# Key weights in blocks of 128 rows, first sums on two engines, and a new order for a transformer layer on one core

## The chip, the cores and the metric

The kernel runs on one core of a Trainium2 chip. The metric is the device time of one execution in microseconds (us); lower is better. The engines are TensorE (PE in the profile), VectorE (DVE), ScalarE (ACT), GpSimd (POOL) and SyncE (SP). SP, and here at the start ACT too, issue the DMAs that move data between the chip's main memory and the on-chip buffers; a name with q behind it, such as SPq, is the queue of that engine.

## The reference

A layer normalisation, an attention whose features are softmaxes, an output projection with a residual, and a gated feed-forward with a second residual, on x of 2048 rows and 448 columns in bf16:

```python
# A: x is layer-normalised first; 16 heads of 28
q, k, v = heads(x @ wqkv)
pq, pk = q @ w_phi, k @ w_phi                    # per head
phi_q = concat(softmax(pq), softmax(-pq))        # 28 + 28 features
phi_k = concat(softmax(pk), softmax(-pk))
kv, z = sum_s phi_k v, sum_s phi_k
o = (phi_q kv) / (phi_q z + 1e-6)
h = x + o @ wo
# B: h is layer-normalised first
h2 = h + (sigmoid(hn @ w_gate) * (hn @ w_up)) @ w_down     # 1792 inner columns
```

## The kernel before

The 2048 rows are 16 tiles of 128 rows (t = 0 to 15), or eight pairs of tiles (pr). All work is cut into named tasks. Each task has an engine, or a short list of engines that may run it, a function that issues its instructions, and the names of the tasks that it needs. A planner would order them by cost, but here the order is written out: `ORDER` is a table of some 900 numbers. The number divided by 32 is the place of a task among all tasks as they are declared; the last two bits choose among the task's engines, and three bits in between choose PSUM banks. `stored` decodes the table, and `emit` gives each engine its tasks in that order, with a semaphore wait wherever a task needs a result of another engine. So each engine, and each DMA queue, works strictly in its own order, and a task that waits holds all that stands behind it on its engine.

The stages, with the task names used below:

- Loads. `x,t` loads tiles of x (two or four at a time), `wk` the key weights, `wph` the feature weights, `wv` the value weights, `wq` the query weights (four pieces), `wom` the output weights (eight pieces). `wg`, `wu`, `wd` are the feed-forward weights and come later, each waiting for the one two places earlier.
- Weights. `kT` transposes the key weights on PE (four tasks of four transposes, line 537), `WkT` copies each result out of PSUM, `wM,1` multiplies it with the feature weights `Wp` (line 553), and `W2,1` casts the folded key weights back. The query weights go the same way, but their transpose is a DMA (`wqT`, line 499), followed by `wM,0` and `W2,0`.
- Normalisation of x. `bst` (line 581) and `agg` are the statistics, `ve` and `rstd` the inverse deviation (the power runs on POOL), `mm` and `nm` a helper for ACT, `xn` (lines 600 and 601) writes the normalised tile. Tiles 0 to 3 are transposed on PE (`xP`, line 611) and copied (`xT`); the others, in pairs, by DMA (`xT`, line 619, on SP).
- Keys and values. `pa` and `pb` are the two parts of a tile's key and value products (line 635; for tiles 0 and 1 the value products are `va`, `vb`). `ekp` and `ekm` are exponentials on ACT (lines 655, 657), `v1` copies the values. `sa` (line 665) adds the two halves of the exponentials' features in each group, from 896 to 448 elements in f32; `ss` sums further, `rs` inverts, `phi` (line 681) scales. `kv` adds the tile's part to a PSUM bank that `kv0` starts.
- Queries: `qa`, `q` (line 733) and the exponentials `eqp`, `eqm` (line 743), for 512 rows at a time.
- After `kvz`, which masks the finished sums: `num` (line 769), its copy `ocp`, then `rSm`, `rr`, `b`, `c`, `rd`, `o` on DVE for a pair, the transposes `oT` (by DMA on SP, line 818, behind `od`, or for pair 0 on PE as `oP`), the projection `woa`, `wo_` (line 830), the residual (`h`, or `hc` for pair 0, whose residual is added in PSUM by `wr`), the second statistics, `hn`, and its transposes `hT`.
- Feed-forward in five chunks of 2, 4, 4, 4 and 2 tiles: `ga`, `gu` (line 931), `sig` on ACT, `hh` on DVE, `dn` (line 965), `fin` and the store `st`.

At the start PE has nothing to do while data comes. It then runs `fill` tasks, matmuls of zeros (line 985). There are 17, and `ORDER` places them: 13 ahead of the first transposes and four between the later ones. The key weights arrive as one load of four blocks of 112 rows:

```python
load("wk", wk_raw[:], A_wqkv[:, D:2 * D].rearrange("(a p) n -> p a n", p=GP), bias=BIG, size=392.0,
     engs=("act", "sp"))
```

Of the kernel before, what the change touches and what calls it, by code (L numbers as in the profile page):

```python
# [5 lines left out]
dt = mybir.dt  # L6
# [4 lines left out]
P = 128  # L11
D = 448
H = 16
DH = 28
G = 4
HL = 4
GP = 112
KT = 4
# [13 lines left out]
NWARM = 1  # L32
NFILL = 17
# [62 lines left out]
class _Graph:  # L96
# [29 lines left out]
    def opt(self, name):  # L126
        return name if name in self.tasks else None
# [194 lines left out]
def build(nc, A_x, A_wqkv, A_w_phi, A_wo, B_w_gate, B_w_up, B_w_down, out):  # L322
# [16 lines left out]
    NXP, NEK, NPHI, NV, NOP, NO, NHP, NSG, NSA = 8, 4, 3, 4, 3, 2, 2, 4, 2  # L339
    SPLIT = range(NT)  # L340

    with ExitStack() as es:
# [8 lines left out]
        WkT = sb("WkT", [P, KT, D])  # L351
# [10 lines left out]
        ident = sb("ident", [P, P])  # L362
# [5 lines left out]
        warm = sb("warm", [P, P])  # L368
# [29 lines left out]
        o_pad = sb("o_pad", [P, NO, 2, 512])  # L398
        oT = sb("oT", [P, NO, 2, G, P])
        wk_raw = nc.alloc_sbuf_tensor_at("wk_raw", [GP, G, D], dt.bfloat16, offset=nc.lookup_mloc(o_pad).addr)  # L400
# [7 lines left out]
        bank16 = {b: a.bitcast(dt.bfloat16) for b, a in bank.items()}  # L408
# [3 lines left out]
        task, opt = K.task, K.opt  # L412
# [47 lines left out]
        def load(name, dst, src, eng="sp", deps=(), bias=0.0, size=0.0, behind=(), engs=None):  # L460
            task(name, eng, 0.55 if eng == "sp" else 0.6, lambda e: e.dma_start(dst, src), deps, lat=0.9, kind="in",
                 bias=bias, size=size, behind=behind, engs=engs)
# [7 lines left out]
        BIG = 2000.0  # L470
# [7 lines left out]
        def rows_of(w, c0, n, half_):  # L478
# [4 lines left out]
        load("wk", wk_raw[:], A_wqkv[:, D:2 * D].rearrange("(a p) n -> p a n", p=GP), bias=BIG, size=392.0,  # L483
             engs=("act", "sp"))
        load("wph", wphd[:], A_w_phi.rearrange("h i j -> (h i) j").rearrange("(a p) j -> p a j", p=GP), bias=BIG - 1,
             size=30.0)
        for h_ in range(2):
            load(("wv", h_), Wv[:, 2 * h_:2 * h_ + 2, :], rows_of(A_wqkv, 2 * D, D, h_), bias=BIG - 4 - h_, size=224.0,
                 engs=("act", "sp"))
# [43 lines left out]
        for b in range(G):  # L533
            def f(e, b=b):
                bk = got(("kT", b))[0]
                for k in range(G):
                    r = e.transpose(bank16[bk][0:GP, k * GP:(k + 1) * GP], wk_raw[:, k, b * GP:(b + 1) * GP],
                                    ident[0:GP, 0:GP])
                return r
            task(("kT", b), "pe", 0.3, f, ["wk", "ident", ("warm", NWARM - 1)], banks=ANY, until=[("WkT", b)], bias=950.0)  # L540
            task(("WkT", b), None, dve(D), lambda e, b=b: copy(
                e, WkT[0:GP, b, :], bank16[got(("kT", b))[0]][0:GP, 0:D]), [("kT", b)], bias=940.0,
                engs=("act", "dve") if b % 2 == 0 else ("dve", "act"))
# [109 lines left out]
        for t in range(NT):  # L653
# [10 lines left out]
            if t in SPLIT:  # L664
                task(("sa", t), "pool", 0.88, lambda e, t=t, s=s: e.tensor_tensor(  # L665
# [3 lines left out]
                    [("ekp", t), ("ekm", t), opt(("ss", t - NSA))])  # L669
# [356 lines left out]
```

## Time and profile before

| what | value |
|---|---|
| median of 3 runs | 208.35 us (208.34 to 208.68) |
| the profiled execution | 208.78 us, of which the span of the profile is 207.0 us |
| PE busy | 198.2 us, 96% of the span |
| DVE busy | 138.5 us, 67% |
| ACT busy | 94.9 us, 46% |
| POOL busy | 34.2 us, 16% |
| first key product (line 635) | starts at 12.35 us |
| mask of the finished sums, `kvz` | starts at 49.49 us |
| first feed-forward product (line 931) | starts at 67.77 us |
| last PE work ends | about 204.1 us |

The span is the stretch between the first and the last recorded event; the remaining 1.78 us of the profiled execution lie around it. A busy share is a mean over stages that differ: DVE, at 67%, is busy 4.9 of every 5 us between 5 and 40 us. PE counts the fillers as busy. In a timeline row the first number is the start, the second the duration of the row (of all its instructions, where an `x` and a count follow), and brackets give the idle time before it with what ended that.

### The profile page before, as it was taken

The page shows a single profiled execution, that of the slowest core. Times are in us where ns is not written, and L with a number is a line of the kernel's source. Part 1 is how long each engine was busy: PE and PEld are TensorE (multiplying, and loading weights), DVE is VectorE, ACT ScalarE, POOL GpSimd, SP SyncE. Part 2 cuts the span into 40 slices and gives each one's busy share as a digit, 9 for nine tenths or more (in the row PEclk, how much of TensorE's full clock was granted, in tenths as well). Part 3 has the DMA queues.
Part 4 walks back from the last instruction along what each step waited for, and adds up shares of the span by engine and source line. Part 5 has one row for each costly group of instructions (what it writes and reads, how often), then busy time and mean ns, then how long its engine had stood idle before and what let it go on. Part 6 is the DMA issues. An engine that isn't in the chain of part 4 may idle for free.

```text
span 207.0 us, 5437 instructions
## 1 busy us (share of the span) xinstructions
PE 198.2 (96%) x2281; PEld 106.6 (51%) x2281; DVE 138.5 (67%) x318; ACT 94.9 (46%) x166; POOL 34.2 (16%) x56
## 2 busy tenths in 40 slices
PE   7799988999898999999999999999999999999994
PEld 2444545555444887444444444544444455796553
DVE  2999999987999999379895655434744332462042
ACT  2399799889998944343411234003243320252000
POOL 5628763740001030002100101000100000000000
PEclk9999999999999999999999999999999999999999
DMA  6989896953027568600722000700050000000043
GB/s 189 288 155 150 176 222 165 232 182 92 3 51 54 73 134 155 118 0 19 130 52 54 0 3 8 144 1 3 2 139 3 0 2 3 0 3 0 3 142 124
DMA packets 35093, 16.94 MB, mean 82 GB/s; under 512 B 26812, under 2 KB 34044, under 8 KB 35068
## 3 DMA queue, kind: packets, MB, share of 16 engines
q1 hardware_dynamic: 34332, 15.96, 36.9%
q10 hardware_dynamic: 736, 0.63, 1.0%
q8 instruction: 18, 0.29, 0.6%
q14 instruction: 7, 0.06, 0.1%
HBM read 8.98 MB, written 1.84 MB: 52 GB/s over the span
## 4 chain that ended last, share of the span: by engine, by line
PE 72%; DVE 15%; DMA 6%; ACT 3%; issue 1%; POOL 1%; POOLq 0%; ACTq 0%
PE bank L931 38%; PE bank L965 18%; PE bank L635 6%; DMA oT<-o_pad 5%; PE bank L830 3%; PE bank L733 3%; DVE st L581 2%; PE bank L693 2%; DVE xn_pad L601 2%; DMA x_sb<-in_A_x_dram 2%; DVE phi L681 1%; DVE o_pad L797 1%; DVE b_sb L792 1%; DVE b_sb L789 1%; PE bank L769 1%
## 5 line engine op out<-in xcount | busy, mean ns | idle before, releaser
L931 PE MATMUL bank<-xnT,wg_sb 64*128 64x512 bf16 (+1 forms) x490 | 87.7, 333 | 0.0
L931 PE MATMUL bank<-xnT,wu_sb 64*128 64x512 bf16 (+1 forms) x490 | 87.7, 333 | 0.0
L940 ACT ACTIVATE sg_sb<-bank 128x512 f32<-128x512 f32 (+1 forms) x70 | 34.6, 511 | 82.7 <-PE bank L931 78.2
L948 DVE SCALAR_TENSOR_TENSOR hh<-sg_sb,bank 128x512 bf16<-128x512 f32 (+1 forms) x70 | 39.2, 575 | 34.7 <-ACT sg_sb L940 34.4
L931 PEld LDWEIGHTS bank<-xnT,wg_sb 64*128 64x128 bf16 x490 | 45.3, 94 | 20.1 <-issue 1.4
L931 PEld LDWEIGHTS bank<-xnT,wu_sb 64*128 64x128 bf16 x490 | 45.1, 94 | 16.8
L965 PE MATMUL bank<-wd_sb,hh 128*128 128x448 bf16 (+1 forms) x238 | 43.1, 342 | 0.0
L965 PEld LDWEIGHTS bank<-wd_sb,hh 128*128 128x128 bf16 x238 | 22.9, 98 | 20.1 <-issue 1.1
L972 DVE SCALAR_TENSOR_TENSOR x_sb<-bank,x_sb 128x448 bf16<-128x448 f32 (+1 forms) x17 | 9.8, 594 | 23.1 <-PE bank L965 23.1
L635 PE MATMUL bank<-Wk,xnT 64*128 64x448 bf16 x112 | 21.5, 350 | 0.1
L635 PE MATMUL bank<-Wv,xnT 64*128 64x448 bf16 x112 | 21.2, 350 | 0.0
L870 POOL TENSOR_TENSOR rs<-rs,neghalf 128x2 f32<-128x2 f32 x8 | 6.4, 805 | 87.4 <-DVE rs L868 87.2
L665 POOL TENSOR_TENSOR half_s<-ek 128x448 f32<-128x448 bf16 x16 | 16.7, 1056 | 13.8 <-ACT ek L657 6.0
L743 ACT ACTIVATE eq<-bank 128x1024 bf16<-128x1024 f32 x16 | 16.6, 1041 | 1.2 <-PE bank L733 0.9
L733 PE MATMUL bank<-xnT,Wq 64*128 64x512 bf16 x112 | 14.6, 377 | 0.8 <-DVE opm L425 0.5
L830 PE MATMUL bank<-wo_sb,oT 64*128 64x448 bf16 x112 | 13.3, 350 | 0.9 <-DMA oT<-o_pad 0.6
L425 ACT CAST opm<-bank 128x960 bf16<-128x960 f32 x14 | 13.1, 979 | 0.9 <-PE bank L769 0.8
L635 PEld LDWEIGHTS bank<-Wk,xnT 64*128 64x128 bf16 x112 | 9.4, 94 | 5.7 <-PE bank L635 0.5
L635 PEld LDWEIGHTS bank<-Wv,xnT 64*128 64x128 bf16 x112 | 9.4, 94 | 5.1 <-ACT ek L657 0.3
L581 DVE BATCH_NORM_STATS2 st<-x_sb 128x6 f32<-128x448 bf16 x16 | 9.3, 608 | 1.8 <-DMA x_sb<-in_A_x_dram 1.8
L681 DVE TENSOR_TENSOR phi<-ek,rsum 128x896 bf16<-128x896 bf16 x16 | 10.1, 653 | 0.1
L670 DVE TENSOR_REDUCE ssum<-half_s 128x32 f32<-128x448 f32 x16 | 9.7, 608 | 0.6 <-POOL half_s L665 0.5
(91 smaller groups left out, 177.6 us busy)
## 6 DMA issues: line engine op xcount, KB each, us to landing
wu_sb<-in_B_w_up_dram SPq DMA_DIRECT2D x4, 448.0 KB, 3.6
wg_sb<-in_B_w_gate_dram SPq DMA_DIRECT2D x4, 448.0 KB, 4.7
out_dram<-x_sb SPq DMA_DIRECT2D x15, 112.0 KB, 1.8
wd_sb<-in_B_w_down_dram SPq DMA_DIRECT2D x7, 224.0 KB, 3.6
x_sb<-in_A_x_dram SPq DMA_DIRECT2D x2, 448.0 KB, 5.6
x_sb<-in_A_x_dram SPq DMA_DIRECT2D x3, 224.0 KB, 4.2
wq_raw<-in_A_wqkv_dram SPq DMA_DIRECT2D x4, 128.0 KB, 5.1
Wv<-in_A_wqkv_dram SPq DMA_DIRECT2D x2, 224.0 KB, 5.2
```

The source lines that it names most:

```text
L425: return e.copy(dst, src) if hasattr(e, "activation") else e.tensor_copy(dst, src)
L581: task(("bst", t), "dve", dve(D), lambda e, t=t: e.bn_stats(st1[:, t % 4, :], X(t)), [x_ld[t], opt(("agg", t - 4))])
L635: r = e.matmul(bank[bk][:, 0:D], lhsT=half(xnT, hi)[:, t, k, :], rhs=half(w, hi)[:, k, :], start=(i == 0), stop=(i == 6), tile_position=(6 ...
L665: task(("sa", t), "pool", 0.88, lambda e, t=t, s=s: e.tensor_tensor(half_s[:, t % NSA].rearrange("p (a n) -> p a n", a=4 * G), ek[:, s].re ...
L681: task(("phi", t), None, 1.68, lambda e, t=t, s=s: e.tensor_tensor(phi[:, t % NPHI, :, :, 0:DH, :].rearrange("p a g d h -> p (a g) d h"), ...
L733: r = e.matmul(bank[bb[j]], lhsT=half(Wq2, hi)[:, k, 2 * g:2 * g + 2].rearrange("p c d h -> p (c d h)"), rhs=half(xnT, hi)[:, 4 * c:4 * c ...
L743: task((key, gp, c), "act", act_p(1024), lambda e, gp=gp, c=c, sg=sg, nm=nm: e.activation(eq[c][:, sg, 2 * gp:2 * gp + 2, :], wide[got(nm) ...
L830: r = e.matmul(bank[bb[j]][:, 0:D], lhsT=half(oT, hi)[:, pr % NO, j, k, :], rhs=half(wo_sb, hi)[:, k, :], start=(i == 0 and not res), stop ...
L931: r = e.matmul(bank[b][:, 0:N], lhsT=half(w, hi)[:, k, fs], rhs=half(hnT, hi)[:, t0:t0 + n, k, :], start=(i == 0), stop=(i == 6), tile_pos ...
L940: task(("sig", f_, c), "act", act_p(N), lambda e, j=j, N=N, nm=nm: e.activation(sg_sb[:, j % NSG, 0:N], bank[got(nm)[0]][:, 0:N], ACT.Tanh ...
L948: task(("hh", f_, c), "dve", dve(N), lambda e, j=j, N=N, nm=nm, f_=f_, c=c: e.scalar_tensor_tensor(hhT[c % 2][:, f_, 0:N], sg_sb[:, j % NS ...
L965: r = e.matmul(bank[b][:, c0:c1], lhsT=hhT[c % 2][:, f_, o:o + P], rhs=wd_sb[:, f_, c0:c1], start=(f_ == 0), stop=(f_ == FT - 1))
```

## The change

The key weights are loaded in blocks of 128 rows: three blocks in one load and the remaining 64 rows in a second. The tile `wk_raw` gets 128 partitions, and each `kT` transposes blocks of 128, 128, 128 and 64 rows instead of four of 112. `sa` may run on POOL or on DVE. `NFILL` falls from 17 to 14. `ORDER` is a new table, with new choices of engine.

```diff
-NFILL = 17
+NFILL = 14
...
-704 545 0 96 224 1120 320 736 352 576 28384 256 608 28416 480 384 28448 768 448 288 28480 800 128 160 28512
+544 576 0 480 1152 609 224 737 128 28416 160 640 96 28448 352 801 192 28480 768 256 448 28512 384 896 28544
...
-        wk_raw = nc.alloc_sbuf_tensor_at("wk_raw", [GP, G, D], dt.bfloat16, offset=nc.lookup_mloc(o_pad).addr)
+        wk_raw = nc.alloc_sbuf_tensor_at("wk_raw", [P, KT, D], dt.bfloat16, offset=nc.lookup_mloc(o_pad).addr)
...
-        load("wk", wk_raw[:], A_wqkv[:, D:2 * D].rearrange("(a p) n -> p a n", p=GP), bias=BIG, size=392.0,
-             engs=("act", "sp"))
+
+        load(("wk", 0), wk_raw[:, 0:3, :], A_wqkv[0:3 * P, D:2 * D].rearrange("(a p) n -> p a n", p=P), bias=BIG,
+             size=336.0, engs=("act", "sp"))
+        load(("wk", 1), wk_raw[0:64, 3, :], A_wqkv[3 * P:D, D:2 * D], bias=BIG, size=56.0, engs=("act", "sp"))
...
-                for k in range(G):
-                    r = e.transpose(bank16[bk][0:GP, k * GP:(k + 1) * GP], wk_raw[:, k, b * GP:(b + 1) * GP],
-                                    ident[0:GP, 0:GP])
+                for k in range(KT):
+                    m = min(P, D - k * P)
+                    r = e.transpose(bank16[bk][0:GP, k * P:k * P + m], wk_raw[0:m, k, b * GP:(b + 1) * GP], ident[0:m, 0:m])
...
-                task(("sa", t), "pool", 0.88, lambda e, t=t, s=s: e.tensor_tensor(
+                task(("sa", t), None, 0.88, lambda e, t=t, s=s: e.tensor_tensor(
...
-                    [("ekp", t), ("ekm", t), opt(("ss", t - NSA))])
+                    [("ekp", t), ("ekm", t), opt(("ss", t - NSA))],
+                    engs=("pool", "dve"))
```

What the new table does to the queues at the start, in the order of issue:

| queue | before | after |
|---|---|---|
| ACT, loads | `x,0`; `wk` | `wk,0`; `x,2`; `x,6` |
| SP, loads | `x,2`, `x,4`, `wph`, `x,6`, `x,8`, `wv,0`, `wq,2`, `wq,0`, `wom,3`, `wv,1`, `x,12` | `x,0`, `wk,1`, `wph`, `x,4`, `wq,0`, `wq,3`, `x,8`, `wq,2`, `wv,0`, `wv,1`, `wq,1`, `x,12` |
| SP, next | `xT,4`, `wq,3`, `wom,0`, `wq,1`, `xT,6`, `wqT,1`, `wqT,0`, `xT,8` | `wqT,1`, `wom,4`, `wqT,0`, `xT,4`, `xT,6`, `xT,8` |
| PE | 13 fillers, `xP,1`, `kT,0`, `kT,2`, `kT,1`, `xP,2`, `kT,3`, the four `wM,1` with one filler, `xP,0`, `xP,3`, three fillers, `pa,0` | 12 fillers, the four `kT`, `xP,1`, three `wM,1`, `xP,0`, `kv0`, the last `wM,1`, two fillers, `xP,2`, `xP,3`, `pa,0` |

Four of the 16 `sa` (tiles 6, 10, 12 and 15) are on DVE after the change. Other tasks change sides too: `W2,1,2`, `W2,0,1`, `W2,0,2`, `v1` of tiles 8, 9, 12 and 14, `xn` of tiles 6, 10 and 12 and the two `hT` copies of pair 0 go from DVE to ACT; `xT,1`, `v1` of tiles 0, 5 and 10 and `xn` of tiles 13 and 14 go from ACT to DVE. Lines behind the edits move by two or three: line 635 becomes 637, line 931 becomes 934.

More of the change, by code (lines that the diff above doesn't have):

```diff
@@ L535, in f @@
                 bk = got(("kT", b))[0]
-                for k in range(G):
-                    r = e.transpose(bank16[bk][0:GP, k * GP:(k + 1) * GP], wk_raw[:, k, b * GP:(b + 1) * GP],
-                                    ident[0:GP, 0:GP])
+                for k in range(KT):
+                    m = min(P, D - k * P)
+                    r = e.transpose(bank16[bk][0:GP, k * P:k * P + m], wk_raw[0:m, k, b * GP:(b + 1) * GP], ident[0:m, 0:m])
                 return r
-            task(("kT", b), "pe", 0.3, f, ["wk", "ident", ("warm", NWARM - 1)], banks=ANY, until=[("WkT", b)], bias=950.0)
+            task(("kT", b), "pe", 0.3, f, [("wk", 0), ("wk", 1), "ident", ("warm", NWARM - 1)], banks=ANY, until=[("WkT", b)], bias=950.0)
             task(("WkT", b), None, dve(D), lambda e, b=b: copy(
```

92 rows, old and new, of the table ORDER are left out of this document.

## The prediction

> **What bounds the kernel now.** I read the page first (engine shares by slice), then the timeline of each engine over the first 70 us, the waits of TensorE (PE), and the DMA issues with their landing times. 0.2% of the time, 0.42 us, is about what a measurement of this kernel can tell from no change.
>
> ```profile
> PE   7799988999898999999999999999999999999994
> DVE  2999999987999999379895655434744332462042
> ```
>
> These are slices of 5.2 us. From 68 us on PE is full (its 136 us of feed-forward work are the same instructions before and after). Earlier VectorE (DVE) is just as full, so time can only come from the first 68 us, and there from two engines at once. PE's timeline, start and duration in us:
>
> ```profile
> 1.44 5.71 PE L985 MATMUL bank<-warm 128*128 128x512 bf16 x13
> 7.90 0.40 PE L611 MATMUL bank<-ident,xn_pad 128*128 128x128 bf16 x4 [0.74 <-DVE xn_pad L601]
> 8.13 0.78 PE L537 MATMUL bank<-ident,wk_raw 112*112 112x112 bf16 x12
> 12.35 0.93 PE L635 MATMUL bank<-Wk,xnT 64*128 64x448 bf16 x8
> ```
>
> Fillers run to 7.15. PE then waits for the normalised tile 1, because its transpose stands ahead of the key weights' in the queue; the weights start at 8.13 and the first key product at 12.35. The weights themselves were issued at 1.29 and landed 5.4 later, at 6.69:
>
> ```profile
> wk_raw<-in_A_wqkv_dram ACTq DMA_DIRECT2D x1, 392.0 KB, 5.4
> ```
>
> From the waits of PE:
>
> ```profile
> PE bank L693 <- DVE phi L681: 1.0, 2, 0.6
> PE bank L553 <- DVE Wq L425: 0.5, 1, 0.5
> ```
>
> These are the stalls between 12.35 and the end of the key/value stage at 49.4: 0.40 at 21.92, 0.53 at 27.07, 0.60 at 31.65, together 1.53 us. Behind them stand delays of DVE:
>
> ```profile
> 19.07 2.32 POOL L665 TENSOR_TENSOR half_s<-ek 128x448 f32<-128x448 bf16 x2 [0.32 <-ACT ek L657]
> 19.50 1.06 DVE L601 TENSOR_SCALAR xn_pad<-x_sb,mv,rs 128x512 bf16<-128x512 bf16 x1
> 36.39 1.86 DVE L681 TENSOR_TENSOR phi<-ek,rsum 128x896 bf16<-128x896 bf16 x2
> ```
>
> A normalisation takes 0.40 alone and 1.06 here, while GpSimd (POOL) adds halves (`sa`). It recurs at 24.17 (+0.76), 29.17 (+0.64) and in the pair at 36.39 (1.86 against 1.10): 2.8 us of DVE in all. Last, the transposes of x by DMA on SP's queue:
>
> ```profile
> 12.95 1.33 SPq L619 DMA_TRANSPOSE xnT<-xn_pad  x1
> 18.68 2.86 SPq L499 DMA_TRANSPOSE WqT<-wq_raw  x2
> DMA to landing us min/median/max: 3.1/4.5/4.8
> ```
>
> The first one issued at 12.95 feeds the product of tile 4, which ran at 18.16 without a wait.
>
> **The change, part by part.**
>
> *Key weights and fillers.* `wk` becomes two loads. The built order puts the first (336 KB) at the head of ScalarE's (ACT) queue, but the second (56 KB) on SP's, behind `x,0`. On ACT's queue 630 KB before (`x,0`, `wk`) had landed at 6.69; now 344 KB at its head should land near 5.0. That alone buys nothing: `wk` was already in 0.46 before the old fillers ended. Twelve fillers instead of 13 stand ahead, at 0.43 each: PE is free at 6.7 instead of 7.15. What counts is that the four `kT` now stand ahead of `xP,1`: they start at 6.7, not 8.13 (1.4 earlier). The number of transposes and their columns are the same, up to 128 wide instead of 112, so their cost stays.
>
> *Up to the first key product.* ACT: four `WkT` copies (1.84) 7.0 to 8.9, four `W2` casts (0.48 each, one of them from DVE) to 10.8. DVE: `x,0` lands at 4.1 as the first load on SP did before, then 7 statistics at 0.54, 4 aggregations at 0.15, 4 normalisations at 0.37, one 0.17, and `xT,1` at 0.40 (now here, not on ACT): 6.4, plus 0.3 of waits for `x,2` and `x,6`, which now come behind `wk` (estimates 6.3 and 7.8 from the 630 KB at 6.69), so `xT,0` ends at 11.1. First product at 11.25 instead of 12.35: **-1.1**; bounds 10.9 (no wait for x) and 12.1 (`x,6` at 8.5 and no overlap).
>
> *Transposes on SP.* Both `wqT` (1.43 each to issue) now stand ahead of `xT,4`; `wqT,0` waits for `wq,1`, which lands near 12.1 (the first batch of some 3.0 MB was in by 12.2, when DMA fell idle; `wq,1` now stands ahead of its last 448 KB), so SP is free at about 13.4. That hides, because `xn,5`, which `xT,4` needs, comes later: DVE after 11.1 does a statistic, four aggregations, one 0.17, three statistics, one 0.16 and two normalisations, 3.6 in all: 14.7 against 12.95 before. Landing 4.7 later: 19.4. PE gets there at 18.2: 11.25 plus the products of tiles 0 to 3 (5.25), three query folds (0.8) and one `kv` (0.3), with 0.6 of waits for ACT's `ekm,3` and for `phi,0`. Old progress there: 18.16 plus the folds and the `kv`, 1.1, is 19.26; so the lead of 1.1 turns into 0.14 behind: **+1.2**; bounds 0.6 (landing after 4.1) and 2.2 (DVE held once more by POOL). Queued behind it on PE: `wM,0,3`, tiles 5 to 7. The later transposes gain: `xT,6` at 16.1 (17.32) and `xT,8` at 20.3 (21.64), since the `wqT` are out of their way.
>
> *First sums on either engine.* Four of 16 `sa` (tiles 6, 10, 12, 15) go to DVE: 448 elements there take 0.54 by the statistic's spacing (bounds 0.27, half of `phi`'s spacing for 896, and 0.62): +2.1 on DVE. Against that, over the key/value stage, DVE gives away `W2,1,2`, `W2,0,1`, `W2,0,2`, four `v1` (seven at 0.54), and a net handful of small ones, and takes `xT,1`, three `v1`: the sum is 41.5 us of DVE work before (16 each of statistics 0.54, aggregations 0.13, `ss` 0.53, `rs` 0.30 and `phi` 0.54, 10 normalisations at 0.36, 8 copies at 0.53, 1.0 of small ones) and 41.3 after. ACT gains 2.3 net; it had 3.7 idle between 15 and 50. POOL loses 4.2. With 12 `sa` left on POOL the 2.8 of delays would scale to 2.1.
>
> *Stalls.* With the weights folded earlier (`W2,0` on ACT) and `phi` no longer last, I take the three old stalls as gone: **-1.5**. The delays by POOL do not vanish, they fall elsewhere: **+0.5** on the path (0 to 1.5, what they cost before). [...]
>
> *Numerators to feed-forward.* On DVE `o,1` and `od,1` (0.75) move ahead of `oT`; the two `hT` copies (0.8) go to ACT. By the rows the feed-forward starts 18.4 after the mask `kvz`, 18.28 before: **+0.1** (0 to 0.6).
>
> *Feed-forward.* Same work; `oT,4` now has 4.5 us of PE work between its issue and its use (5.8 before), `oT,5` 4.5 (5.2), against landings of 3.1 to 4.8: **+0.15** (0 to 0.8). The tail keeps its order (two halves of tile 15): 0.
>
> Sum: -1.1 + 1.2 - 1.5 + 0.5 + 0.1 + 0.15 = **-0.65**. The profiled execution took 208.78 (span 207.0 and 1.78 around it), 0.43 above the median of 208.35. So a profiled run near 208.1 and a median of 207.7.
>
> **The rivals.**
>
> *DVE swallows it.* DVE carries 41.3 of work against 41.5 from the same start at 4.1; if the POOL delays stay at 2.8 and 0.6 of new waits come, `kvz` stays at 49.5 and the time at 208.35. For: DVE's slices are all 9s. Against: four fewer `sa` on POOL, and the waits of 0.29 and 0.54 late in the stage went with them. Chance 0.17.
>
> *The late transpose.* `xT,4` lands at 20.4 or later: `xn,5` meets the first `sa` on POOL (by my walk they start within 0.2 of each other), or the wire is still full, since `wq,1` and `wq,3` join the first batch. Then the wait is 2.2 or more and moves all products of tiles 4 to 7. With half of the old stalls left: -1.1 + 2.2 - 0.75 + 0.5 + 0.1 + 0.15 = +1.1, 209.4. It decides from a landing of about 20.0. Chance 0.22.
>
> *A slow TensorE.* The fillers start every 0.43, but four transposes take 0.40 at 7.90: PE was at half rate up to at least 6.6 and at full rate by 7.9. With fewer fillers the transposes and folds could run at half rate, +1.7 of PE work before and 1.3 in the first product: -0.65 + 1.3 = 209.0. The page's clock row (all 9s) does not show it. Chance 0.06. [...] Here 5.5 us of fillers had passed and the spacing was still 0.43.
>
> *Order in the feed-forward.* Two late `oT` cost over 1 us: 209.0. Chance 0.07.
>
> *All of the lead is kept.* `xT,4` early, no delay by POOL: -1.1 + 0.6 - 1.5 + 0.1 = -1.9, 206.45. Chance 0.10.
>
> **How the numbers follow.** The forecast has the remaining 0.38. Faster: 0.38 + 0.10 = 0.48; same 0.17; slower 0.22 + 0.06 + 0.07 = 0.35. Both signs hold much, so the forecast's own range is 207.1 to 207.9. The range of all, 206.4 to 209.4, runs from the kept lead to the late transpose; beyond it lie sums with several bad ends at once.
>
> **What would show it.** Right: `kT` at about 6.7, first L635 (now L637) near 11.25, a PE wait of about 1.2 before tile 4, no waits on `Wq`, the feed-forward's first matmul near 67.0 (67.77). Wrong: first product after 12.1, `xT,4` issued after 15.5, DVE normalisations still above 1 us four times or more, or PE gaps after 70 us. Halves added on DVE taking more than 0.7 would spoil the third part.

## The result, and the profile after

The changed kernel takes 207.54 us in the median of 20 runs (207.21 to 209.07), the kernel before 208.5 in the runs beside it (208.07 to 209.83). The ratio is 0.996 (95% interval 0.9947 to 0.9972). The profiled execution took 207.67, with a span of 205.9 (208.78 and 207.0 before).

The page's slices first, as before in steps of 5.2 us: PE is a little fuller in the second and sixth slice and a little emptier near 50 us; DVE is about as full as it was up to 60 us.

```profile
PE   7899998998988999999999999999999999999993
DVE  2999999997998996789823875435446415351241
```

PE's timeline at the start (start, duration). The transposes of the key weights start at 6.35 instead of 8.13 but take 1.91; PE then waits for the normalised tile 1 all the same, and the first key product starts at 11.76 (12.35 before):

```profile
1.43 4.60 PE L988 MATMUL bank<-warm 128*128 128x512 bf16 x12
6.35 1.91 PE L540 MATMUL bank<-ident,wk_raw 128*112 128x128 bf16 x16 [0.32 <-issue]
8.88 0.40 PE L613 MATMUL bank<-ident,xn_pad 128*128 128x128 bf16 x4 [0.61 <-DVE xn_pad L603]
9.93 0.36 PE L703 MATMUL bank<-zsel,epsT 128*128 128x464 bf16 x1
11.76 1.74 PE L637 MATMUL bank<-Wk,xnT 64*128 64x448 bf16 x14
```

DVE's work starts with the landing of `x,0`, which came 0.36 later than before (DVE's timelines, before and then after). Counted from it, the first key product came 8.25 later before and 7.30 later now:

```profile
4.10 1.15 DVE L581 BATCH_NORM_STATS2 st<-x_sb 128x6 f32<-128x448 bf16 x2 [1.82 <-DMA x_sb<-in_A_x_dram]
4.46 0.63 DVE L583 BATCH_NORM_STATS2 st<-x_sb 128x6 f32<-128x448 bf16 x1 [1.67 <-DMA x_sb<-in_A_x_dram]
```

What held tile 1 (an operation that takes longer than alone while POOL works is called held here; the locks in two of the expectations are the same delays), first from POOL's timeline, then from DVE's: the two `Wp` began 0.51 ahead of `xn,1`, which took 1.03 instead of 0.40. The last two rows are the two such holds that are left in the key/value stage:

```profile
7.28 1.08 POOL L524 TENSOR_TENSOR Wp<-wphd,maskW 112x224 bf16<-112x224 bf16 x2
```

```profile
7.79 1.03 DVE L603 TENSOR_SCALAR xn_pad<-x_sb,mv,rs 128x512 bf16<-128x512 bf16 x1
28.81 1.06 DVE L603 TENSOR_SCALAR xn_pad<-x_sb,mv,rs 128x512 bf16<-128x512 bf16 x1
31.57 1.87 DVE L684 TENSOR_TENSOR phi<-ek,rsum 128x896 bf16<-128x896 bf16 x2
```

PE's waits between the first key product and the mask (in all, times, longest), 0.85 against 1.53 before:

```profile
PE bank L696 <- DVE phi L684: 0.6, 1, 0.6
PE bank L637 <- ACT Wq L425: 0.3, 1, 0.3
```

Then the transpose of tiles 4 and 5 on SP's queue (the row holds `xT,4` and `xT,6`), the landing time of the first of them, and, from PE's timeline, the first product of tile 4, with no wait in front of it:

```profile
15.16 2.88 SPq L621 DMA_TRANSPOSE xnT<-xn_pad  x2
```

```profile
DMA to landing us min/median/max: 3.4/3.4/3.4
```

```profile
19.00 0.36 PE L637 MATMUL bank<-Wk,xnT 64*128 64x448 bf16 x1
```

Last the mask (DVE) and the first feed-forward product (PE):

```profile
48.68 0.64 DVE L751 TENSOR_TENSOR kvz<-bank,dmask 128x464 bf16<-128x464 f32 x1 [0.88 <-PE bank L696]
```

```profile
66.45 0.27 PE L934 MATMUL bank<-xnT,wu_sb 64*128 64x256 bf16 x1
```

| | before | after | difference |
|---|---|---|---|
| first key product | 12.35 | 11.76 | -0.59 |
| from there to `kvz` | 37.14 | 36.92 | -0.22 |
| from there to the feed-forward | 18.28 | 17.77 | -0.51 |
| from there to the end of the span | 139.23 | 139.45 | +0.22 |
| span | 207.0 | 205.9 | -1.1 |

### The profile page after: what moved, and what is told of

Its sections match the earlier page's. It is cut to its first block, busy times and chain, and to the rows that moved or that the text cites. A ratio compares the mean times of both kernels' runs of the same rounds, so it can differ in the third digit from the quotient of the medians.

```text
span 205.9 us, 5431 instructions
## 1 busy us (share of the span) xinstructions
PE 197.2 (96%) x2278; PEld 107.1 (52%) x2278; DVE 135.6 (66%) x312; ACT 96.5 (47%) x172; POOL 30.6 (15%) x56
## 4 chain that ended last, share of the span: by engine, by line
PE 78%; DVE 12%; ACT 4%; DMA 2%; issue 1%; POOL 1%
PE bank L934 42%; PE bank L968 21%; PE bank L637 5%; PE bank L833 4%; PE bank L736 3%; DMA x_sb<-in_A_x_dram 2%; DVE phi L684 2%; PE bank L696 1%; DVE ssum L673 1%; DVE xn_pad L603 1%; DVE st L583 1%; ACT xn_pad L602 1%; ACT ek L659 1%; DVE b_sb L792 1%; DVE b_sb L795 1%
## 5 line engine op out<-in xcount | busy, mean ns | idle before, releaser
L637 PE MATMUL bank<-Wk,xnT 64*128 64x448 bf16 x112 | 22.1, 350 | 0.4 <-ACT Wq L425 0.3
L871 POOL TENSOR_SCALAR rs<-mv 128x2 f32<-128x2 f32 x5 | 1.3, 256 | 99.6 <-DVE mv L869 50.3
L667 POOL TENSOR_TENSOR half_s<-ek 128x448 f32<-128x448 bf16 x12 | 12.9, 1078 | 15.3 <-ACT ek L657 7.0
L425 ACT CAST opm<-bank 128x960 bf16<-128x960 f32 x14 | 13.7, 1014 | 2.8 <-PE bank L772 2.1
L736 PE MATMUL bank<-xnT,Wq 64*128 64x512 bf16 x112 | 14.0, 377 | 0.1
L657 ACT ACTIVATE ek<-bank 128x448 bf16<-128x448 f32 x16 | 9.7, 630 | 1.3 <-PE bank L637 1.3
```

The costliest lines, as they stand in the source:

```text
L425: return e.copy(dst, src) if hasattr(e, "activation") else e.tensor_copy(dst, src)
L637: r = e.matmul(bank[bk][:, 0:D], lhsT=half(xnT, hi)[:, t, k, :], rhs=half(w, hi)[:, k, :], start=(i == 0), stop=(i == 6), tile_position=(6 ...
L667: task(("sa", t), None, 0.88, lambda e, t=t, s=s: e.tensor_tensor(half_s[:, t % NSA].rearrange("p (a n) -> p a n", a=4 * G), ek[:, s].rear ...
L736: r = e.matmul(bank[bb[j]], lhsT=half(Wq2, hi)[:, k, 2 * g:2 * g + 2].rearrange("p c d h -> p (c d h)"), rhs=half(xnT, hi)[:, 4 * c:4 * c ...
```

## The experiments

Times are medians; each ratio is to the kernel before, run beside it, with its 95% interval. Order edits are written as queues. All marks are in one table at the end of this section.

**new_start and new_rest: the new order cut in two at the first key product.**

```diff
 new_start: ORDER = changed order up to pa,0, then the order and engines before
 new_rest:  ORDER = order before up to pa,0, then the changed order and engines
```

> The changed kernel's order up to the first key product, then the order and the engines of the kernel before (all first sums on POOL). Theory S (the start pays, the stalls behind it are only moved): in the changed kernel PE idles 3.5 us between 12 and 68 us, against 3.6 before, while the first key product is 0.59 earlier and the 0.37 of kv0 lies ahead of it instead of behind; so nearly all of the 1.1 us of span comes from the start, and this kernel should take 207.6 (207.3 to 207.9), with its first key product near 11.8. Rival L (the ledger of the prediction: the rest of the order removes 1.5 us of stalls, the start's lead is lost at tile 4): 208.3 or more. Rival D (VectorE sets the end of the key/value stage): the mask kvz stays near 49.4 and the time near 208.4.

> The kernel before up to the first key product (one load of the key weights, 17 fillers), then the changed kernel's order and engines, with four first sums on VectorE. Theory S: 208.4 (208.1 to 208.7), the first key product near 12.35 as before and PE's idle time behind it still near 3.5 us. Rival L: the old stalls (0.40, 0.53, 0.60) go without any lead to lose, 207.5 or less. Rival D: between the two, about 208.0.

Measured: new_start 210.0 (1.0093, 1.0079 to 1.0107), new_rest 208.88 (1.0032, 1.0020 to 1.0043). Both are slower than either whole kernel, so the two halves do not add. Theory S misses new_rest by 0.2 only, but new_start by 2.1. L's "208.3 or more" takes in new_start, but not for L's reason: PE did not wait ahead of tile 4 there. D holds in neither. new_start is not a clean cut either: its first key product came 7.78 behind the landing of `x,0`, not 7.30, with 0.4 of waiting for a statistic on DVE. Behind it PE had new waits and DVE a pause in the middle of its fullest stretch (PE's waits, then DVE's timeline):

```profile
PE bank L696 <- DVE phi L684: 2.0, 2, 1.4
PE bank L637 <- ACT ek L659: 0.9, 2, 0.7
```

```profile
13.70 0.16 DVE L593 TENSOR_TENSOR nm<-nm,rs 128x4 f32<-128x4 f32 x1 [1.06 <-POOL rs L588]
```

The new start defers the aggregations, `rstd,4` and `xn,5` behind the first key product, and the old order has nothing to put in front of POOL's power there. In new_rest it is the other way round: the old start does not load all of `wq` in time, and the folds of the query weights wait:

```profile
PE bank L553 <- DMA WqT<-wq_raw: 0.9, 1, 0.9
```

**sums_on_pool and before_sums: the first sums alone, taken out of the change and put into the kernel before.**

```diff
 sums_on_pool: changed kernel, sa of tiles 6, 10, 12, 15
-DVE
+POOL
 before_sums: kernel before, the same four
-POOL
+DVE
```

> The changed kernel with the first sums of tiles 6, 10, 12 and 15 back on POOL, nothing else changed. PE idles only 0.85 us between the first key product and kvz in the changed kernel. Theory S: moving 2.1 us off VectorE can give back at most that, and POOL's longer locks can cost about as much; 207.6 (207.3 to 208.0). Rival P (the sums on either engine are what pays: POOL's delays of VectorE go from 2.0 back to 2.8 us and land on PE): 208.2 or more, with new waits of PE for phi.

> The kernel before with the first sums of tiles 6, 10, 12 and 15 on VectorE and nothing else changed (the part of the change alone). With these four on POOL the changed kernel took 0.2% more. Theory A (a part pays only in the order made for it): VectorE gets 2.1 us more between 12 and 49 us, where it was 95% to 98% busy up to 36 us; the mask kvz moves by less than 0.5 and the time is 208.0 to 208.8 (ratio 0.999 to 1.002). Rival P (POOL's locks are what costs): the stalls for phi go, ratio 0.996 or less. Rival D (VectorE is the bound of the stage): 1.0 to 2.1 us more, ratio 1.005 to 1.01.

Measured: sums_on_pool 207.78 (0.9979, 0.9970 to 0.9988), before_sums 209.22 (1.0049, 1.0035 to 1.0063). In the old order the part costs 1.0 us: DVE is the bound there, as rival D said, at the low end of its range and a hair below its ratio. PE waits longer for `phi`, and `kvz` comes 1.0 later after the first key product (38.18 against 37.14):

```profile
PE bank L694 <- DVE phi L682: 2.0, 3, 1.1
```

In the changed order theory S holds, 207.78 of 207.3 to 208.0: the same part is worth at most 0.2%, and the intervals touch. Without it DVE waits for others where it was full before (DVE's waits in sums_on_pool):

```profile
DVE phi L684 <- ACT ek L657: 1.2, 1, 1.2
DVE ssum L673 <- POOL half_s L667: 0.9, 1, 0.9
```

So in the new order DVE has room for the four sums (that this room comes from the work moved to ACT is argued, not tried), and PE's waits are the same with and without them, but for 0.2 for a late `oT`.

**weights_one_load and one_load_behind: the key weights as one load again, in the changed order.**

```diff
-load(("wk", 0), ...)   # 3 blocks of 128 rows, 336 KB, ACT
-load(("wk", 1), ...)   # 64 rows, 56 KB, SP
+load("wk", ...)        # 4 blocks of 112 rows, 392 KB, ACT
 one_load_behind, ACT's queue:
-wk; x,2; x,6
+wph; wk; x,2; x,6
```

> The changed kernel with the key weights as one load of four blocks of 112 rows at the head of ScalarE's queue, and transposes of 112 rows; the order is otherwise the changed one. In the changed kernel the transposes kT start at 6.35, when the 56 KB piece on SP's queue is in (6.30), 0.32 after the last filler, and xP,1 behind them waits until 8.88 for its normalised tile anyway. Theory S: the form of the load is covered by that wait; kT at 6.0 to 6.6, first key product 11.76 plus or minus 0.1, time 207.55 (207.3 to 207.8). Rival B (blocks of 128 rows are what pays): the weights land later, kT at 7 or later, and the first key product and the time move by 0.4 or more, to 208.0.

> The kernel weights_one_load (one load of 392 KB in blocks of 112 rows) with the 24.5 KB of wph put ahead of it on ScalarE's queue, so that the 392 KB are issued 0.5 later than x,0 on SP's queue. In weights_one_load the first tiles x,0 landed at 5.39 instead of 4.46, with 95 packets of weights and 17 of x moved by 3.0 us; in the changed kernel it was 9 of weights and 129 of x. Theory Q (whichever of the two loads is first on the wire keeps it; the shorter issue, 0.44 against 0.47, put the weights first): x,0 lands at 4.5 or earlier, the first key product starts near 11.5 to 12.0, time 207.6 (ratio 0.996 to 0.998). Rival Y (56 KB more of weights, or their 112 rows, slow x,0 down): x,0 lands after 5.0, time 209.5 or more.

Measured: weights_one_load 210.04 (1.0086, 1.0072 to 1.0100): neither theory S nor rival B. The weights were early (transposes at 5.67), but `x,0` landed at 5.39 and moved DVE's whole chain (the timelines of PE and DVE):

```profile
5.67 1.03 PE L540 MATMUL bank<-ident,wk_raw 112*112 112x112 bf16 x16
```

```profile
5.39 0.63 DVE L584 BATCH_NORM_STATS2 st<-x_sb 128x6 f32<-128x448 bf16 x1 [2.60 <-DMA x_sb<-in_A_x_dram]
```

The DMA view up to 3.0 us shows whose queue went first; q10 is ACT's queue, headed by the weights, q1 is SP's, headed by `x,0` (packets, MB, share; the view does not tell the loads of one queue apart). First the changed kernel, then weights_one_load:

```profile
q1 hardware_dynamic: 142, 0.13, 20.8%
q10 hardware_dynamic: 9, 0.01, 7.4%
```

```profile
q10 hardware_dynamic: 112, 0.10, 27.1%
q1 hardware_dynamic: 17, 0.02, 1.6%
```

Both loads are issued at 0.78; ACT's issue took 0.44 for the one load and 0.49 for the three blocks, SP's 0.46 to 0.47 for `x,0`. In one_load_behind the one load comes 0.5 later, and `x,0` landed at 4.32: theory Q holds for the landing. Its time is not what Q said: 208.45 (1.0007, 0.9987 to 1.0027), because `x,2`, now half a microsecond later on ACT's queue, was late in its turn, PE idled 1.35, and in half of the 12 executions the clock fell (see the last section; in weights_one_load it fell in all five, which is a part of its time). The six at full clock took 207.42 to 208.26, with a median of 207.6, Q's figure.

**features_first: `Wp` out of the way of `xn,1`.**

```diff
 ACT's queue:
-wk,0; x,2; x,6
+wph; wk,0; x,2; x,6
 POOL:
-rstd,0; ve,1; rstd,1; Wp,0; Wp,1
+Wp,0; Wp,1; rstd,0; ve,1; rstd,1
```

> The changed kernel with the feature weights wph as the first load on ScalarE's queue (ahead of wk,0), and the two Wp on POOL ahead of its first power rstd,0; nothing else. In the changed kernel the two Wp run at 7.28 to 8.36, hold xn,1 on VectorE for 1.03 instead of 0.40, and PE waits 0.61 for it with the folds wM,1 behind. Theory H (that hold sets the first key product): xn,1 takes 0.4, the first key product starts at 11.1 to 11.3 (11.76), and the time falls by 0.3 to 0.6, to a ratio near 0.9935 to the kernel before. Rival W (the folded weights or x set it, the hold is covered): first key product 11.6 or later, time unchanged. Rival K (a lead at the start is lost at the later waits, as the hybrid orders suggest): first key product early, time unchanged within 0.2.

Measured: 207.75 (0.9987, 0.9970 to 1.0005), first key product 11.88. The hold went, but a wait for `x,2` of the same kind as in one_load_behind took its place:

```profile
7.27 1.15 DVE L583 BATCH_NORM_STATS2 st<-x_sb 128x6 f32<-128x448 bf16 x2 [1.01 <-DMA x_sb<-in_A_x_dram]
8.55 0.38 DVE L603 TENSOR_SCALAR xn_pad<-x_sb,mv,rs 128x512 bf16<-128x512 bf16 x1
```

So the figures are those of rival W, with `x,2` as what set the product (11.6 or later, time unchanged), and H stays open: the chain of DVE was as long as before.

**fewer_switches: the 64-row block first in two of the four `kT`.**

```diff
-                for k in range(KT):
+                for k in (range(KT) if b in (0, 3) else reversed(range(KT))):
```

> The changed kernel with the 64-row block transposed first instead of last in kT,1 and kT,2, so that TensorE goes from 128 rows to 64 or back four times instead of seven within the 16 transposes. They took 1.91 us in the changed kernel, 1.03 as 16 blocks of 112 rows in weights_one_load. Theory T (each change of row count costs about 0.12): 1.4 to 1.6 us. Rival C (TensorE was still slow at 6.3 to 8.3 us): 1.9 as before. Either way the wait for xn,1 until 8.88 covers it: time unchanged within 0.2 (ratio 0.996).

Measured: 207.34 (0.9961, 0.9948 to 0.9973), the 16 transposes 1.54:

```profile
6.28 1.54 PE L540 MATMUL bank<-ident,wk_raw 128*112 128x128 bf16 x16
```

Theory T: three changes of row count fewer saved 0.37, 0.12 each. In the changed kernel's trace the transposes start 0.055 to 0.07 apart where the row count stays, 0.10 for the second one behind a return to 128 rows, and 0.15 to 0.16 where the row count changes. The saving is off the path, as expected.

**loads_behind: two loads of 448 KB between `xT,4` and `xT,6`.**

```diff
 SP's queue:
-wqT,0; xT,4; xT,6; xT,8
+wqT,0; xT,4; wg,0; wu,0; xT,6; xT,8
```

> The changed kernel with the first two feed-forward loads (448 KB each) issued right behind xT,4 on SP's queue, instead of behind xT,10. In the kernel before, where loads were queued right behind it, xT,4 landed 4.8 after its issue; in the changed kernel, with only xT,6 behind, 3.4. Theory V (the loads behind it share the engines and slow the transpose): xT,4 lands 4.5 to 5.0 after its issue at 15.2, so at about 19.9, PE waits 0.7 to 1.1 ahead of tile 4, and the time rises by 0.4 to 1.0 (ratio about 0.999). Rival N (the landing differs for another reason): 3.4 as before, no wait, ratio 0.996.

Measured: 209.28 (1.0078, 1.0050 to 1.0106), but not by V. `xT,4` landed 3.2 after its issue, as N said; it was `xT,6`, issued 0.5 behind the second load, that took 6.0, and PE waited for it ahead of tile 6:

```profile
23.27 0.36 PE L637 MATMUL bank<-Wk,xnT 64*128 64x448 bf16 x1 [1.98 <-DMA xnT<-xn_pad]
```

Both transposes right behind these two loads were slow (`xT,12` in the changed kernel, behind the same two, took 5.2); the one with them right behind it, in this one run, was not. Why `xT,4` took 4.8 in the kernel before, with DMA idle ahead of it, stays open.

**x_first, mid_edits and both_edits: does a lead at the start reach the end?**

```diff
 x_first = fewer_switches with POOL as in features_first, and the queues
-ACT: wk,0; x,2; x,6          SP: x,0; wk,1; wph; x,4
+ACT: wph; wk,0; x,6          SP: x,0; x,2; wk,1; x,4
 mid_edits = fewer_switches with
-POOL: ve2,0                  DVE: rr,2; od,1; oT,0,1; oT,0,0
+DVE: ve2,0 ahead of b,3      DVE: od,1; oT,0,1; oT,0,0; rr,2
```

> The kernel fewer_switches with wph first on ScalarE's queue and the two Wp on POOL ahead of rstd,0 (as in features_first), and x,2 moved to SP's queue, right behind x,0. In features_first the hold of xn,1 was gone (0.38 instead of 1.03), but x,2, half a microsecond later on ScalarE's queue, landed at 7.27 and VectorE idled 1.01 for it. Theory H (the chain of VectorE from x,0 to xT,0 sets the first key product): x,2 lands by 6.3, no hold, first key product at 10.8 to 11.1 (11.60 in fewer_switches), and the time falls by 0.3 to 0.7, to a ratio of 0.993 to 0.9945. Rival K (a lead at the start goes into later waits): first key product as early, ratio 0.996. Rival Z (the wire: x,2 and wk,0 slow each other): first key product after 11.4, ratio 0.996 or more.

> The kernel fewer_switches with two small moves between the mask kvz and the feed-forward: ve2,0 on VectorE ahead of b,3 instead of on POOL, and rr,2 behind oT,0,0. In fewer_switches POOL's ve2,0 and rstd2,0 take 0.51 and 1.10 beside VectorE's two-input operations, VectorE waits 0.60 and PE 0.49 for hn, and PE waits 0.58 for oT,0,0. Theory M (TensorE is the bound behind the mask, each of its waits is paid): hn 0.3 to 0.5 earlier, oT,0,0 0.1 earlier, the feed-forward starts 0.4 to 0.6 earlier than 66.29, ratio 0.9935 to 0.9945. Rival E (the next wait, for opm or hT on ScalarE, takes their place): less than 0.2, ratio 0.9955 to 0.9965.

> The edits of x_first and of mid_edits together. Theories H and M: the gains add, 0.8 to 1.2 us under the changed kernel, ratio 0.990 to 0.9925. Rivals K, Z and E: the better of the two single ones, no more, ratio 0.994 to 0.996.

Measured: x_first 207.18 (0.9949, 0.9937 to 0.9962), mid_edits 206.98 (0.9941, 0.9929 to 0.9954), both_edits 206.97 (0.9940, 0.9927 to 0.9952). In x_first nothing holds `xn,1` and `x,2` is in time; the first key product starts at 11.19, now behind the last `W2` on ACT:

```profile
7.41 0.38 DVE L603 TENSOR_SCALAR xn_pad<-x_sb,mv,rs 128x512 bf16<-128x512 bf16 x1
```

```profile
11.19 1.73 PE L637 MATMUL bank<-Wk,xnT 64*128 64x448 bf16 x14 [0.38 <-ACT Wk L425]
```

That is 0.41 under fewer_switches and just outside H's 10.8 to 11.1; the medians differ by 0.16 only, less than H's 0.3. Half of the 0.41 is not the edit's: `x,0` landed at 4.09, in fewer_switches at 4.29. Beside loads_behind, with the hold and `x,0` at 4.10, the gain is 0.18 (11.37). PE stood ready at 10.81, 6.72 behind the landing for 7.27 there, but then waited 0.38 for ACT: the twelve fillers ended at 6.77 in this execution (6.03 in the changed kernel's), `kT` began at 6.84 (6.28 in fewer_switches), and ACT's chain from there ended last. So with the hold DVE's chain sets the first key product, as H says; without it ACT's did here, and what the hold costs lies between 0.18 and some 0.55, an estimate from these rows. Rival K falls in the trace: the 0.41, whatever they come from, are still there at `kvz` (48.12 against 48.53) and at the feed-forward (65.88 against 66.29). In mid_edits the normalisation behind the mask no longer waits for POOL (DVE's timeline, fewer_switches and then mid_edits):

```profile
63.60 0.74 DVE L877 TENSOR_SCALAR hn_pad<-x_sb,mv,rs 128x512 bf16<-128x512 bf16 x2 [0.60 <-POOL rs L873]
```

```profile
63.25 0.73 DVE L877 TENSOR_SCALAR hn_pad<-x_sb,mv,rs 128x512 bf16<-128x512 bf16 x2
```

The way from `kvz` to the feed-forward is 17.51 instead of 17.76, so of M's 0.4 to 0.6 some 0.25 came, though the ratio is in M's range. Together the two give 0.66 at the feed-forward (65.63), in the traces about a sum. In the times the sum is not seen: the ratio of both_edits is what rivals K, Z and E said, the better of the two and no more, and its profiled execution was the fastest of its five. Both kernels lie under the changed one, by 0.6 us in the medians and 0.4 by the ratios, but the intervals overlap by 0.0005 and 0.0007, so this is not clear of noise.

| kernel | first key product | to `kvz` | to feed-forward | span | ratio |
|---|---|---|---|---|---|
| before | 12.35 | 37.14 | 18.28 | 207.0 | 1 |
| before_sums | 12.05 | 38.18 | 18.03 | 207.5 | 1.0049 |
| new_start | 12.04 | 39.37 | 17.81 | 208.2 | 1.0093 |
| new_rest | 12.37 | 37.50 | 17.77 | 207.2 | 1.0032 |
| changed | 11.76 | 36.92 | 17.77 | 205.9 | 0.9960 |
| sums_on_pool | 11.45 | 36.96 | 17.76 | 205.9 | 0.9979 |
| features_first | 11.88 | 36.92 | 17.76 | 206.0 | 0.9987 |
| fewer_switches | 11.60 | 36.93 | 17.76 | 205.7 | 0.9961 |
| loads_behind | 11.37 | 38.61 | 17.75 | 207.1 | 1.0078 |
| x_first | 11.19 | 36.93 | 17.76 | 205.5 | 0.9949 |
| mid_edits | 11.49 | 36.94 | 17.51 | 205.3 | 0.9941 |
| both_edits | 11.19 | 36.93 | 17.51 | 205.0 | 0.9940 |

The two one-load kernels are not in the table, because the clock fell in their profiled executions. The table is the main finding. Behind its own start, the new order runs to the mask in 36.92 to 36.96 wherever no load is late, whether the start is at 11.19 or at 11.88. The starts themselves vary with the execution: sums_on_pool and loads_behind have the start of the changed kernel unedited, at 11.45 and 11.37 for 11.76, and in the five kernels with the hold and the changed kernel's loads (changed, sums_on_pool, fewer_switches, loads_behind, mid_edits) the product comes 7.27 to 7.31 behind the landing of `x,0`.

## Why the prediction was right, and where its terms were not

The forecast was -0.65 and 207.7; the span fell by 1.1 and the median by 0.96, and the forecast's own range held it. That the way and the size came out is in good part luck: errors of both signs met. Of the five signs named for being right, the early `kT` came (6.35 for 6.7); the first key product was 0.5 late, the wait ahead of tile 4 was missing, one wait on `Wq` was left (0.28), and the feed-forward came 0.55 early. None of the signs of being wrong came.

- *First key product, -1.1 forecast, -0.59 measured.* Of the 0.51 that is missing, 0.36 is the landing of `x,0`, at 4.46, not 4.1 (4.04 to 4.29 in the profiles of the other kernels with the weights in two loads and the new start, so most of this is spread). From the landing on, the forecast had 7.15 and 7.30 came, and two errors met there as well. The walk of DVE gave `xn,1` the 0.40 of a free normalisation, but it was held by the two `Wp` on POOL, 0.63 more; POOL's delays had been charged to the key/value stage only. The 0.3 of waits for `x,2` and `x,6` did not come. In x_first, without hold and without waits for x, PE stood ready 6.72 behind the landing; of that lead over 7.27, 0.38 went into a wait for ACT.
- *Transposes of the key weights, "their cost stays".* Wrong: 1.91 against 1.03 for 16 transposes of 112 rows (weights_one_load), by the changes of row count. The wait for `xn,1` covers it, so the sum did not suffer. And the start of `kT` hung on the 56 KB on SP's queue, in at 6.30, more than on the fillers; the 336 KB landed at 5.1, as forecast (the prediction's 344 and 630 KB are the 336 and 616 KB of the rows in thousands of bytes).
- *Wait ahead of tile 4, +1.2 forecast, none measured.* The issue was right (15.16 against 14.7), the landing wrong: 4.7 was taken from the one row of before that was 4.8, when that view also held 3.1. It took 3.4, so it landed at 18.56, and PE came at 19.00 instead of 18.2, 0.5 of that from its late start. This is the largest error, and the rival "late transpose" rests on it. loads_behind shows that a late transpose can stop PE (1.98 of waiting, for `xT,6`), there with two loads of 448 KB just ahead of it.
- *Stalls, -1.5 and +0.5 forecast.* 1.53 became 0.85, so -0.7 instead of -1.0. POOL's holds of DVE in that stage were 1.4 (0.65 at 28.81, 0.77 in the pair at 31.57), not 2.1. The delays that the prediction lists are of different operations: normalisations at 19.50 and 29.17, the small `ve` at 24.17 and two `phi` at 36.39. Only `phi` takes two whole tensors; a normalisation takes one, with two columns of scalars. What the rows share is that POOL was adding halves beside each; the `ss` at 22.83 in the kernel before took 0.56 beside one too, no more than elsewhere. Why POOL holds some operations and not others is not shown.
- *Not in the sum at all.* `kv0` (0.36 at 9.93) moved from behind the first key product into the start, where PE was partly idle: -0.37. And `q` products moved ahead of the mask: 48 instead of 56 are behind it, 8 at 0.114 (28 took 3.20), 0.9 more before `kvz` and 0.9 less behind. With them the key/value stage is -0.7 - 0.4 + 0.9 = -0.2, as measured, and the way to the feed-forward -0.9 + 0.6 of longer waits (2.4 against 1.8) = -0.3, of the -0.51 measured; the rest is in pauses too short for the list of waits. The prediction had +0.1 there, and 67.0 for the feed-forward, which began at 66.45.
- *Feed-forward, +0.15 forecast, +0.22 measured.* No wait of PE is listed behind 72 us in either profile, and where the 0.22 lies is open. The other kernels with this order had 139.36 to 139.73 there, so a good part can be spread.
- *First sums on DVE.* 0.61 to 0.63 each, below the 0.7 named as the limit. That they would pay by fewer holds was too simple: alone they cost 1.0 us, and in the new order they are worth at most 0.4.
- *The other rivals.* "DVE swallows it" is what happens without the rest of the order (before_sums). "A slow TensorE" looked true in the trace at first, since the transposes ran at half their pace, but fewer_switches gives the row count as the cause. That fewer fillers would leave PE slow, no run shows: with 12, the last three of the changed kernel's trace started 0.22 apart, not 0.43, like the two at 10.54.

Where the 1.1 us came from, then: by the rows about 0.95 from the start, counting `kv0` that now fits into it, and the rest from slightly shorter waits. Which of the moves at the start shortened it is read from the traces only: no run takes the new start alone without a new wait.

## What to carry to other kernels

Price a moved step by every engine that can hold it, also in the first microseconds, where one operation of 0.4 that is held for 1.0 can sit on the chain that sets the start. Take a transfer's landing time from all its rows, and ask what is queued ahead of it. And before crediting a stage with a gain, count whole work units that cross its boundary: a stage can look slower only because it does more, and here a rigid stage behind the start handed each lead on to the feed-forward. Where the first load's landing varies by 0.4 between executions, compare starts by their distance from it.

## What the runs showed of the hardware

**The first loads raced.** Two loads issued at 0.78 on two queues did not share the wire evenly at first. The queue whose first issue took 0.03 less had 142 of the first 151 packets in the changed kernel, and 112 of 129 in weights_one_load; `x,0` as the loser landed 0.9 later. That the order of issue decides is shown by one_load_behind, where half a microsecond of delay turned the race (`x,0` landed at 4.32 instead of 5.39); that 0.03 is enough is argued from the issue times.

**Row counts on TensorE.** The 16 transposes took 1.91 with seven changes between 128 and 64 rows (changed kernel) and 1.54 with four (fewer_switches), 0.12 a change. With the same four they took 1.55 to 1.69 in both_edits, x_first and mid_edits, which gives 0.07 to 0.12. Blocks of 112 rows, without a change, took 1.03 (weights_one_load). Why a change takes time is not shown.

**The clock fell in kernels with a pause of PE.** The pauses are those of the profiled execution, the counts are executions with a mean granted clock of 0.992 or less. PE idled 3.1 us ahead of tile 1 in weights_one_load, and all five were low; 1.35 in one_load_behind, six of 12; 2.0 ahead of tile 6 in loads_behind, four of 10; 1.4 for `phi` in new_start, one of four; 1.2 in features_first, two of 12; 1.1 in new_rest and before_sums, none of 11; and with 0.9 or less in fewer_switches, x_first, mid_edits, both_edits and sums_on_pool, none of 31. The changed kernel (0.6) had one of 20, its 209.07. The price was 0.7 to 2.2 us where a kernel had both kinds of execution. Only two of the low executions left a trace: in one_load_behind the clock was 0.50 from 9.08 to 12.49, in weights_one_load from 11.08 to 14.50, 3.4 us each. In the other kernels the pause and the fall are put together from different executions, and the profiled one of loads_behind, with its 2.0, kept the full clock; so the length of the pause alone does not decide it. The stretches of one_load_behind show it (columns: stretch, length, busy time of PE, PEld, DVE, ACT, POOL, granted clock, DMA share, GB/s):

```profile
6.00:8.00 2.00, 1.32 (x18) 0.90 (x16) 1.15 (x4) 0.91 (x3) 1.73 (x5) 1.00 1.18 286
8.00:10.00 2.00, 0.98 (x11) 0.98 (x12) 2.00 (x7) 0.92 (x3) 1.55 (x5) 0.77 1.15 299
10.00:12.00 2.00, 2.00 (x18) 1.63 (x17) 2.00 (x7) 1.45 (x4) 0.00 (x0) 0.50 1.16 321
12.00:14.00 2.00, 2.00 (x18) 0.89 (x16) 1.97 (x9) 1.53 (x3) 1.21 (x2) 0.88 1.18 280
```

In one_load_behind the longest pause ahead of the fall was 1.35 (with 0.36 ahead of the weights). Whether fillers in such a pause would have kept the clock up, no run here tries.
